# Attention with a gated feed-forward block on one core: 32-column tiles for values and row sums, batch 0 masked by TensorE, loads and output matmuls moved

## The chip, the cores and the metric

The kernel runs on one core of a Trainium2 chip. The metric is the device time of one execution in microseconds (us). The traces were taken by the hardware profiler; PE is TensorE's matmuls, PEld its weight loads, DVE VectorE, ACT ScalarE, POOL GpSimd, SP SyncE. The granted clock (PEclk in the views) is the share of TensorE's full clock that the profiler records as let through. PSUM is the memory in which the matmuls leave their results, in banks.

## The reference

```python
def _attn_ref(q, k, v, beacon_k, beacon_v):          # B, H, S, Nb, D = 8, 8, 576, 16, 64
    k_all = np.concatenate([beacon_k, k], axis=2)
    v_all = np.concatenate([beacon_v, v], axis=2)
    scores = scale * np.matmul(q, k_all.transpose(0, 1, 3, 2))
    causal[:, Nb:] = np.triu(np.ones((S, S), dtype=bool), k=1)
    scores = np.where(causal, -1e9, scores)
    a = softmax(scores)                              # written out in the original
    return np.matmul(a, v_all)

def _moe_ref(x, w_gate, w_val, w_out):               # x: 4608 x 512, d_ff = 1536
    return (gelu(x @ w_gate) * (x @ w_val)) @ w_out
```

The output of attention, 8 heads of 64 side by side, is `x`. Inputs and output are float32 in memory; the matmuls are in bf16.

## The kernel before

A batch has four pairs of heads. For each pair, the scores are made in four chunks (0 to 3) in a ring of two PSUM buffers; ScalarE takes the exponential of each; GpSimd masks the diagonal. Then TensorE multiplies with the values and, with a tile of ones, makes row sums. After attention, 12 gate/value tiles of 8 matmuls follow. The 48 output matmuls of a batch are those of the chunk of tokens before it, and they are strewn in bursts `o(n)` over attention, to keep TensorE busy while ScalarE works.

```python
    psum_s: bufs=2, two banks each    # scores, gate/value
    psum_x: bufs=1, three banks       # values and row sums; also output tile 0 of a batch
    psum_o: bufs=1, one bank          # output tiles 1, 2 and 3 of a batch
# ... (cut; a summary of the pools, not the code's own lines)

    def out_mms(ci, u0, u1, wide=lambda ti: False):
        for u in range(u0, u1):
            ti, fi = divmod(u, F_TILES)              # F_TILES = 12: an output tile is 12 matmuls
            # ... (cut)
            if fi == 0:
                if wide(ti):
                    o_of[ci][1] = psum_x.tile([P, 1536], FP32, name="o_ps", tag="x")[:, 0:D_MODEL]
                else:
                    o_of[ci][1] = psum_o.tile([P, D_MODEL], FP32, name="o_ps", tag="o")
            # ... (cut: the matmul)
            if fi == F_TILES - 1:
                keep(nc.vector.tensor_copy(o_sb[:, ti, :], o_ps))
                # ... (cut: the store)

    # batches 1 to 7; ab(m): score chunks 0 and 1 of pair m, cd(m): chunks 2 and 3,
    # av(m): values, row sums and normalization
            o(6)
            ab(0)
            o(10)
            cd(0)
            o(8)
            for m in range(1, NPAIR):
                ab(m)
                av(m - 1)
                cd(m)
                o(6 if m < NPAIR - 1 else 5)
            av(3, direct=True)
            o(7)
        # ... (cut)
        for fi in range(F_TILES):
            gate_val(b, fi, kk_late=fi == 0)
```

`keep` holds each engine's instructions to the order written.

The softmax here doesn't subtract the row's maximum and nothing guards it: scores larger than these inputs give would overflow.

## Time and profile before

| | before |
|---|---|
| time, median | 398.4 us (398.1 to 399.1) |
| TensorE busy | 97% of the span |
| one batch (first gate matmul to the next batch's) | 42.2 us |
| gate/value matmuls in it | 20.8 us |
| values and row sums of one pair | 1.56 us |

The first fence is from the page of the kernel before: the span, the busy time of the engines with their share of the span, and the granted TensorE clock in tenths over 40 slices.

```profile
span 396.2 us, 7413 instructions
PE 382.3 (97%) x3046; PEld 185.9 (47%) x3046; DVE 190.5 (48%) x304; ACT 202.2 (51%) x280; POOL 156.3 (39%) x277
...
PEclk9999999999999999999999999999999999999999
...
PE 79%; DMA 8%; POOL 3%; DVE 3%; ACT 3%; issue 2%; SPq 2%; POOLq 0%; ACTq 0%
```

The last line is the chain of waits: four fifths of it is TensorE itself. A window over one batch of the same kernel shows that TensorE does not rest there at all: 42.20 us busy in 42.20 us.

```profile
core 0: us, PE busy (x) PEld busy (x) DVE busy (x) ACT busy (x) POOL busy (x), PEclk, DMA share, GB/s
76.44:118.64 42.20, 42.20 (x338) 20.37 (x337) 21.17 (x33) 23.99 (x33) 21.02 (x38) 1.00 0.99 97
```

### The profile page before, as it was taken

How to read it: one execution, taken by the hardware profiler on the slowest of the kernel's cores; microseconds unless marked ns; L12 is line 12 of the kernel's file. 1: busy time of each engine (PE TensorE's matmuls, PEld its weight loads, DVE VectorE, ACT ScalarE, POOL GpSimd, SP SyncE). 2: the span in 40 equal slices, each digit the busy share in tenths (PEclk: the TensorE clock that was granted, in tenths of full speed). 3: DMA queues.
4: the chain of work that ended last, by engine and by line, in shares of the span. 5: the costliest groups of instructions: out<-in, count | busy, mean ns of one | idle time of the engine just before them, and what ended most of it. 6: DMA issues, size and time to landing. Idle time of an engine off the chain costs nothing.

```text
span 396.2 us, 7413 instructions
## 1 busy us (share of the span) xinstructions
PE 382.3 (97%) x3046; PEld 185.9 (47%) x3046; DVE 190.5 (48%) x304; ACT 202.2 (51%) x280; POOL 156.3 (39%) x277
## 2 busy tenths in 40 slices
PE   3889999999999999999999999999999999999996
PEld 2464545544454445444544455444544455444442
DVE  1393654844375327642673338433754266332332
ACT  2775258634873379336843586347823793332210
POOL 8722395780369124931486047803400240000000
PEclk9999999999999999999999999999999999999999
DMA  7999998699129930996099915991032010000012
GB/s 91 180 206 204 175 132 97 68 169 121 55 36 156 141 79 30 120 156 84 29 107 162 89 55 57 163 137 58 28 89 59 34 45 32 0 0 29 28 53 106
DMA packets 139154, 36.24 MB, mean 91 GB/s; under 512 B 126832, under 2 KB 134512, under 8 KB 139120
## 3 DMA queue, kind: packets, MB, share of 16 engines
q0 software_dynamic: 103984, 19.14, 64.4%
q1 hardware_dynamic: 35136, 16.62, 19.3%
q8 instruction: 24, 0.39, 0.4%
q14 instruction: 10, 0.08, 0.1%
HBM read 38.27 MB, written 9.44 MB: 120 GB/s over the span
## 4 chain that ended last, share of the span: by engine, by line
PE 79%; DMA 8%; POOL 3%; DVE 3%; ACT 3%; issue 2%; SPq 2%; POOLq 0%; ACTq 0%
PE gv_ps L155 36%; PE o_ps L155 23%; PE x_ps L155 11%; PE s_ps L155 8%; DMA qkT<-k_sb_94 3%; DMA v_sb_98<-in_beacon_v_dram 2%; SPq L196 2%; ACT expT L158 2%; DMA k_sb_97<-in_k_dram 2%; POOL k_sb_97 L109 1%; PE t_ps L167 1%; DVE qkT L178 1%; POOL q_sb_96 L109 1%; PE w_ps L155 1%; DMA kb<-in_beacon_k_dram 1%
## 5 line engine op out<-in xcount | busy, mean ns | idle before, releaser
L158 ACT ACTIVATE ge_sb<-gv_ps 128x512 bf16<-128x512 f32 x108 | 64.5, 597 | 150.7 <-PE gv_ps L155 150.7
L340 DVE TENSOR_TENSOR hT_sb<-gv_ps,ge_sb 128x512 bf16<-128x512 f32 x108 | 74.7, 692 | 116.0 <-ACT ge_sb L158 116.0
L158 ACT ACTIVATE expT<-s_ps 128x1024 bf16<-128x1024 f32 (+3 forms) x128 | 103.9, 870 | 25.8 <-PE s_ps L155 25.7
L155 PE MATMUL gv_ps<-xT_sb,wg_sb 128*128 128x512 bf16 x432 | 112.2, 379 | 0.8 <-DVE xT_sb L312 0.8
L155 PE MATMUL gv_ps<-xT_sb,wv_sb 128*128 128x512 bf16 x432 | 112.2, 379 | 0.0
L238 POOL TENSOR_SCALAR_AFFINE_SELECT expT<-expT 128x256 bf16<-128x256 bf16 (+2 forms) x140 | 52.4, 388 | 142.2 <-ACT expT L158 142.1
L155 PE MATMUL o_ps<-wo_sb,hT_sb 128*128 128x512 bf16 x432 | 103.6, 380 | 0.0
L155 PEld LDWEIGHTS <-wv_sb 128*128 128x128 bf16 x432 | 42.3, 98 | 52.7 <-issue 2.7
L155 PEld LDWEIGHTS <-wg_sb 128*128 128x128 bf16 x432 | 41.9, 98 | 49.9
L155 PEld LDWEIGHTS <-hT_sb 128*128 128x128 bf16 x432 | 38.8, 98 | 46.6 <-issue 2.8
L364 DVE COPY o_sb<-o_ps 128x512 f32<-128x512 f32 x36 | 24.7, 687 | 37.9 <-PE o_ps L155 37.9
L155 PE MATMUL s_ps<-qkT 64*128 64x80 bf16 (+5 forms) x384 | 39.1, 294 | 2.7 <-DVE qkT L183 1.5
L155 PE MATMUL x_ps<-expT,ones 128*64 128x432 bf16 (+1 forms) x558 | 41.2, 243 | 0.0
L304 DVE STREAM_TRANSPOSE zT_sb<-x_ps 128x576 f32<-128x576 f32 x29 | 22.7, 781 | 29.9 <-ACT x_sb L158 29.9
L155 PEld LDWEIGHTS <-qkT 64*128 64x128 bf16 x384 | 14.8, 96 | 30.4 <-issue 21.8
L155 PEld LDWEIGHTS <-ones 128*64 128x64 bf16 (+1 forms) x578 | 23.2, 110 | 4.6
L307 DVE STREAM_TRANSPOSE rec_sb<-r_sb 128x576 f32<-128x576 f32 x29 | 22.6, 778 | 1.0
L155 PE MATMUL x_ps<-expT,v_sb_95 128*64 128x80 bf16 (+5 forms) x270 | 21.5, 245 | 1.5 <-DVE zT_sb L304 1.1
L155 PE MATMUL x_ps<-expT,v_sb_98 128*64 128x80 bf16 (+5 forms) x288 | 22.8, 246 | 0.0
L109 POOL DMA_DIRECT2D v_sb_98<-in_v_dram x20 | 17.0, 868 | 11.9 <-DMA wv_sb<-in_moe_w_val_dram 3.7
L109 POOL DMA_DIRECT2D v_sb_95<-in_v_dram x20 | 17.0, 889 | 2.5 <-DMA k_sb_94<-in_k_dram 2.3
L312 DVE TENSOR_TENSOR xT_sb<-x_sb,rec_sb 128x576 bf16<-128x576 f32 x23 | 17.4, 758 | 0.9
(51 smaller groups left out, 190.9 us busy)
## 6 DMA issues: line engine op xcount, KB each, us to landing
out_dram<-o_sb SPq DMA_DIRECT2D x36, 256.0 KB, 2.0
v_sb_95<-in_v_dram POOLq DMA_DIRECT2D x12, 128.0 KB, 7.9
wg_sb<-in_moe_w_gate_dram POOLq DMA_DIRECT2D x3, 512.0 KB, 11.6
wv_sb<-in_moe_w_val_dram POOLq DMA_DIRECT2D x3, 512.0 KB, 13.3
wo_sb<-in_moe_w_out_dram POOLq DMA_DIRECT2D x1, 1536.0 KB, 23.5
v_sb_98<-in_v_dram POOLq DMA_DIRECT2D x12, 128.0 KB, 10.6
q_sb_93<-in_q_dram POOLq DMA_DIRECT2D x12, 128.0 KB, 4.2
q_sb_96<-in_q_dram POOLq DMA_DIRECT2D x12, 128.0 KB, 4.2
```

What stands on the lines that cost most here:

```text
L109: keep(nc.gpsimd.dma_start(out=out_ap, in_=in_ap))
L155: keep(nc.tensor.matmul(out_ap, lhsT, rhs, start=start, stop=stop, **kw))
L158: keep(nc.scalar.activation(out_ap, in_ap, func, **kw))
L167: keep(nc.tensor.transpose(out_ap, in_ap, ident[0:n, 0:n]))
L178: nc.vector.tensor_copy(qkT[:, m, :, NB:SK].rearrange("p w (t r) -> p w t r", r=6), t_ps[:, 0:2, 0:S].rearrange("p w (r t) -> p w t r", r=6),)
L196: nc.sync.dma_start_transpose(out=qkT[:, :, w, c + j * P : c + j * P + n], in_=src[0:n, j, :, :].rearrange("p h d -> p (h d)"),)
L238: nc.gpsimd.affine_select(out=d, in_=d, pattern=[[0, 2], [1, n]], compare_op=ALU.is_ge, fill=0.0, base=NB if t == 0 else 0, channel_multip ...
L304: keep(nc.vector.transpose(zT_sb, z_ps))
L307: nc.vector.transpose(rec_sb.rearrange("p (c o) -> p c o", o=32), r_sb.to_broadcast([P, S // 32, 32]))
L312: nc.vector.tensor_tensor(out=xT_sb[:, m, b * S : (b + 1) * S], in0=x_sb, in1=rec_sb, op=ALU.mult)
L340: nc.vector.tensor_tensor(out=h_of[ci][:, fi, :], in0=gv_ps[:, 1, :], in1=ge_sb, op=ALU.mult)
L364: keep(nc.vector.tensor_copy(o_sb[:, ti, :], o_ps))
```

## The change

Its intent, as the code shows it:

- Row sums need only 32 columns of ones, so four 32-column tiles are meant to work at once on two heads and two ranges of queries. Values use four 32-column tiles too. Row sums get a bank of their own (`psum_z`), and the division reads values from PSUM, without ScalarE's copy.
- The rows of `x` are then in another order, so the gate and value weights are loaded in quarters, 24 loads in place of 6, and the third pair of weights comes after batch 1's queries and keys.
- Batch 0: TensorE adds a large negative number above the diagonal; VectorE's masks and ten warming matmuls go.
- The last two gate/value tiles of a batch do both gates first, so that the GELUs end sooner.
- The output matmuls are shared out anew: 14, not 24, before the second pair.

```diff
+ZS = 352
+Z_ORDER = [(0, 0), (0, 1), (1, 1), (1, 0), (2, 1), (2, 0), (3, 1), (4, 1)]
...                                                  (row sums, batches 1 to 7)
+            for t, u in Z_ORDER:
+                lo, end = (ZS, S) if u else (0, ZS)
+                for hi in range(2):
+                    p0 = 64 * u + 32 * hi
+                    mm(z_ps[p0 : p0 + 32, q0 - lo : end - lo], ones[0 : KROWS[t], 0:32], ...)
...                                                  (values: r = 0 to 3, 32 columns each)
+                for r in range(4):
+                    mm(x_ps[32 * r : 32 * r + 32, X0 + q0 : X0 + q1], v_sb[..., 32 * (r // 2) : 32 * (r // 2) + 32], ...)
...                                                  (loads)
-    for i in range(3):
-        load_gate_val(i)
+    load_gate_val(0)
+    load_gate_val(1)
     load_qk6(1, 0, H)
     load_kb(1)
+    load_gate_val(2)
     load_out_w()
...                                                  (batches 1 to 7)
+            o(4)
+            ab(0)
             o(6)
-            ab(0)
-            o(10)
             cd(0)
-            o(8)
+            o(4)
             for m in range(1, NPAIR):
                 ab(m)
                 av(m - 1)
                 cd(m)
-                o(6 if m < NPAIR - 1 else 5)
-            av(3, direct=True)
-            o(7)
+                o(8)
+            av(3)
+            o(10)
...                                                  (gate/value)
-            gate_val(b, fi, kk_late=fi == 0)
+            if fi < F_TILES - 2:
+                gate_val(b, fi, kk_late=fi == 0)
+            elif fi == F_TILES - 2:
+                gate_val_pair(b, fi)
```

(Cut: the masks of batch 0, the order of its pairs, and the normalization's four small reciprocals.)

More of the change, by code (lines that the diff above doesn't have):

```diff
@@ L38 @@
 AV_ORDER = [0, 2, 4, 1, 3]
-X0 = 16
-Z0 = X0 + S
+X0 = 512 - S_LO[4]
+ZS = 352
+Z_ORDER = [(0, 0), (0, 1), (1, 1), (1, 0), (2, 1), (2, 0), (3, 1), (4, 1)]
 QK_SCALE = 0.125
@@ L77 @@
     psum_x = ctx.enter_context(tc.tile_pool(name="psum_x", bufs=1, space=bass.MemoryType.PSUM))
+    psum_z = ctx.enter_context(tc.tile_pool(name="psum_z", bufs=1, space=bass.MemoryType.PSUM))
     psum_o = ctx.enter_context(tc.tile_pool(name="psum_o", bufs=1, space=bass.MemoryType.PSUM))
@@ L100 @@
     nc.vector.memset(qkT[:, :, 1, SK:640], 0.0)
-    tri = const.tile([P, P], BF16, name="tri", tag="tri")
-    nc.vector.memset(tri, 3e38)
+    behind = const.tile([P, P], BF16, name="behind", tag="behind")
+    nc.vector.memset(behind, -3e38)
     def dma(out_ap, in_ap):
@@ L148, in load_gate_val @@
         for w, dst in ((moe_w_gate, wg_sb), (moe_w_val, wv_sb)):
-            keep(nc.gpsimd.dma_start(out=dst[:, :, fs], in_=w[:, fs].rearrange("(kk p) f -> p kk f", p=P)))
+            for g in range(4):
+                a, c = g % 2, g // 2
+                dma(
+                    dst[32 * g : 32 * g + 32, :, fs],
+                    w[:, fs].rearrange("(kk q p) f -> q p kk f", q=4, p=32)[2 * a + c],
+                )
     def load_out_w():
@@ L161, in transpose_pe @@
     def transpose_pe(b, m, pool, tag):
-        t_ps = pool.tile([P, 3 if tag == "x" else 2, 1024], BF16, name="t_ps", tag=tag)
+        t_ps = pool.tile([P, 2, 1024], BF16, name="t_ps", tag=tag)
         qk, kb = qk6[b]
@@ L183, in transpose_pe @@
         keep(nc.vector.tensor_copy(qkT[:, m, 1, 0:NB], t_ps[:, 1, S:SK]))
-    def warm(b, m, n):
-        w_ps = psum_o.tile([P, D_MODEL], FP32, name="w_ps", tag="o")
-        for _ in range(n):
-            mm(w_ps, ident, qkT[:, m, 1, 0:512], True, True)
     def transpose_dma(b):
@@ L209, in scores @@
         s_ps = psum_s.tile([P, 2, 512], FP32, name="s_ps", tag="s")
-        for t, s_lo, w, col in CHUNKS[c]:
+        for j, (t, s_lo, w, col) in enumerate(CHUNKS[c]):
             for hi in range(2):
@@ L216, in scores @@
                     qkT[r, m, 0, NB + s_lo : NB + s_lo + w],
+                    j == 0,
                     True,
-                    True,
+                    skip_group_check=True,
                 )
+        if b == 0:
+            for t, s_lo, w, col in CHUNKS[c]:
+                if s_lo == S_LO[t]:
+                    n, q0 = DIAG[t], NB if t == 0 else 0
+                    for hi in range(2):
+                        mm(
+                            s_ps[:, hi, col : col + n],
+                            behind,
+                            ident[:, q0 : q0 + n],
+                            False,
+                            True,
+                            skip_group_check=True,
+                        )
         o, w = CHUNK_OFF[c], CHUNK_W[c]
@@ L231, in masks @@
             d = expT[0 : KROWS[t], :, EXP_OFF[t] : EXP_OFF[t] + n]
-            if b == 0:
-                w = tri[0 : KROWS[t], NB : NB + n] if t == 0 else tri[0 : KROWS[t], 0:n]
-                w = w.rearrange("p (o n) -> p o n", o=1).to_broadcast([KROWS[t], 2, n])
-                keep(nc.vector.tensor_tensor(out=d, in0=d, in1=w, op=ALU.min))
-            else:
-                keep(
-                    nc.gpsimd.affine_select(
-                        out=d,
-                        in_=d,
-                        pattern=[[0, 2], [1, n]],
-                        compare_op=ALU.is_ge,
-                        fill=0.0,
-                        base=NB if t == 0 else 0,
-                        channel_multiplier=-1,
-                    )
-                )
@@ L251 @@
-    x_of = {}
-    def attend(b, m, t, wide=False):
-        i = b * NPAIR + m
-        if t == AV_ORDER[0]:
-            if wide:
-                x_of[i] = tuple(
-                    (psum_s.tile([P, 1024], FP32, name=name, tag="s"), 0, 512) for name in ("xs_ps", "zs_ps")
-                )
-            else:
-                x_ps = psum_x.tile([P, 1536], FP32, name="x_ps", tag="x")
-                x_of[i] = ((x_ps, X0, 512 - X0), (x_ps, Z0, 1024 - Z0))
-        expT, v_sb = exp_of[i], v_ring[b % NRING]
-        kr, first, last = KROWS[t], t == AV_ORDER[0], t == AV_ORDER[-1]
-        for w, (ps, base, split) in enumerate(x_of[i]):
-            for q0, q1 in ((S_LO[t], split), (max(split, S_LO[t]), S)):
+            keep(
+                nc.gpsimd.affine_select(
+                    out=d,
+                    in_=d,
+                    pattern=[[0, 2], [1, n]],
+                    compare_op=ALU.is_ge,
+                    fill=0.0,
+                    base=NB if t == 0 else 0,
+                    channel_multiplier=-1,
+                )
+            )
@@ new lines, with attend @@
+    x_of = {}
+    def attend(b, m, x_in, by_act):
+        i = b * NPAIR + m
+        expT, v_sb = exp_of[i], v_ring[b % NRING]
+        if by_act:
+            z_ps = psum_s.tile([P, 1024], FP32, name="z_ps", tag="s")
+            for t in AV_ORDER:
+                for q0, q1 in ((S_LO[t], 512), (max(512, S_LO[t]), S)):
+                    e0 = EXP_OFF[t] + q0 - S_LO[t]
+                    for r in range(4):
+                        mm(
+                            z_ps[32 * r : 32 * r + 32, q0:q1],
+                            ones[0 : KROWS[t], 0:32],
+                            expT[0 : KROWS[t], r % 2, e0 : e0 + q1 - q0],
+                            t == AV_ORDER[0],
+                            t == AV_ORDER[-1],
+                            skip_group_check=True,
+                        )
+        else:
+            z_ps = psum_z.tile([P, 512], FP32, name="z_ps", tag="z")
+            for t, u in Z_ORDER:
+                lo, end = (ZS, S) if u else (0, ZS)
+                q0 = max(lo, S_LO[t])
+                e0 = EXP_OFF[t] + q0 - S_LO[t]
+                for hi in range(2):
+                    p0 = 64 * u + 32 * hi
+                    mm(
+                        z_ps[p0 : p0 + 32, q0 - lo : end - lo],
+                        ones[0 : KROWS[t], 0:32],
+                        expT[0 : KROWS[t], hi, e0 : e0 + end - q0],
+                        t == 0,
+                        t == (4 if u else 2),
+                        skip_group_check=True,
+                    )
+        pool, tag = x_in
+        x_ps = pool.tile([P, 1024], FP32, name="x_ps", tag=tag)
+        for t in AV_ORDER:
+            for q0, q1 in ((S_LO[t], S_LO[4]), (max(S_LO[4], S_LO[t]), S)):
@@ L269, in attend @@
                 e0 = EXP_OFF[t] + q0 - S_LO[t]
-                for hi in range(2):
+                for r in range(4):
                     mm(
-                        ps[64 * hi : 64 * hi + 64, base + q0 : base + q1],
-                        ones[0:kr, :] if w else v_sb[0:kr, t, 2 * m + hi, :],
-                        expT[0:kr, hi, e0 : e0 + q1 - q0],
-                        first and (wide or not (w == 1 and q0 == 0)),
-                        last,
+                        x_ps[32 * r : 32 * r + 32, X0 + q0 : X0 + q1],
+                        v_sb[0 : KROWS[t], t, 2 * m + r % 2, 32 * (r // 2) : 32 * (r // 2) + 32],
+                        expT[0 : KROWS[t], r % 2, e0 : e0 + q1 - q0],
+                        t == AV_ORDER[0],
+                        t == AV_ORDER[-1],
@@ L277, in attend, with normalize @@
                         skip_group_check=True,
                     )
-    def normalize(b, m, by_act=False, direct=False):
+        x_of[i] = x_ps[:, X0 : X0 + S], z_ps
+    def normalize(b, m, by_act):
         i = b * NPAIR + m
-        (x_ps, xc, _), (z_ps, zc, _) = x_of.pop(i)
-        x_ps, z_ps = x_ps[:, xc : xc + S], z_ps[:, zc : zc + S]
+        x_ps, z_ps = x_of.pop(i)
         del exp_of[i]
         rec_sb = npool.tile([P, S], FP32, name="rec_sb", tag="rec_sb")
-        x_sb = x_ps
-        if not direct:
-            x_sb = npool.tile([P, S], FP32, name="x_sb", tag="x_sb")
@@ L293, in normalize @@
         if by_act:
-            ln_sb = npool.tile([P, S], FP32, name="ln_sb", tag="zT_sb")
-            act(ln_sb, z_ps, ACT.Ln)
-            if not direct:
-                keep(nc.vector.tensor_copy(x_sb, x_ps))
+            ln_sb = npool.tile([P, S], FP32, name="ln_sb", tag="ln_sb")
+            act(ln_sb, z_ps[:, 0:S], ACT.Ln)
             act(rec_sb, ln_sb, ACT.Exp, scale=-1.0)
         else:
-            zT_sb = npool.tile([P, S], FP32, name="zT_sb", tag="zT_sb")
+            zT_sb = npool.tile([P, ZS], FP32, name="zT_sb", tag="zT_sb")
@@ L301, in normalize @@
             r_sb = npool.tile([P, S // 32, 1], FP32, name="r_sb", tag="r_sb")
-            if not direct:
-                act(x_sb, x_ps, ACT.Copy)
-            keep(nc.vector.transpose(zT_sb, z_ps))
-            keep(nc.vector.reciprocal(r_sb, zT_sb.rearrange("p (c o) -> p c o", o=32)[:, :, 0:1]))
+            n, w = ZS // 32, S - ZS
+            keep(nc.vector.transpose(zT_sb[:, 0:w], z_ps[:, 0:w]))
+            keep(nc.vector.transpose(zT_sb[0:64, w:ZS], z_ps[0:64, w:ZS]))
+            z = zT_sb.rearrange("p (c o) -> p c o", o=32)[:, :, 0:1]
@@ L306, in normalize @@
+            for p in (64, 0):
+                keep(nc.vector.reciprocal(r_sb[p : p + 64, n:, :], z[64:P, 0 : w // 32, :]))
+            for p in (0, 64):
+                keep(nc.vector.reciprocal(r_sb[p : p + 64, 0:n, :], z[0:64, :, :]))
             keep(
@@ L312, in normalize @@
             nc.vector.tensor_tensor(
-                out=xT_sb[:, m, b * S : (b + 1) * S], in0=x_sb, in1=rec_sb, op=ALU.mult
+                out=xT_sb[:, m, b * S : (b + 1) * S], in0=x_ps, in1=rec_sb, op=ALU.mult
             )
@@ L318, with feed_tile, gv_mm, gelu @@
     h_of, o_of = {}, {}
-    def gate_val(ci, fi, kk_late=False):
+    def feed_tile(ci, fi):
         if fi == 0:
             h_of[ci] = hpool.tile([P, F_TILES, CH], BF16, name="hT_sb", tag="hT_sb")
-        n0 = ci * CH
-        gv_ps = psum_s.tile([P, 2, CH], FP32, name="gv_ps", tag="s")
-        order = [(w, kk) for w in range(2) for kk in range(K_CHUNKS)]
-        if kk_late:
-            order.sort(key=lambda t: t[1] == K_CHUNKS - 1)
-        for w, kk in order:
-            mm(
-                gv_ps[:, w, :],
-                (wg_sb, wv_sb)[w][:, kk, fi * P : (fi + 1) * P],
-                xT_sb[:, kk, n0 : n0 + CH],
-                kk == 0,
-                kk == K_CHUNKS - 1,
-                skip_group_check=True,
-            )
+        return psum_s.tile([P, 2, CH], FP32, name="gv_ps", tag="s")
+    def gv_mm(gv_ps, ci, fi, w, kk):
+        mm(
+            gv_ps[:, w, :],
+            (wg_sb, wv_sb)[w][:, kk, fi * P : (fi + 1) * P],
+            xT_sb[:, kk, ci * CH : (ci + 1) * CH],
+            kk == 0,
+            kk == K_CHUNKS - 1,
+            skip_group_check=True,
+        )
+    def gelu(gv_ps):
         ge_sb = fpool.tile([P, CH], BF16, name="ge_sb", tag="ge_sb")
         act(ge_sb, gv_ps[:, 0, :], ACT.Gelu)
+        return ge_sb
+    def product(ci, fi, gv_ps, ge_sb):
         keep(
@@ L343, in gate_val, with gate_val_pair @@
         )
+    def gate_val(ci, fi, kk_late=False):
+        gv_ps = feed_tile(ci, fi)
+        order = [(w, kk) for w in range(2) for kk in range(K_CHUNKS)]
+        if kk_late:
+            order.sort(key=lambda t: t[1] == K_CHUNKS - 1)
+        for w, kk in order:
+            gv_mm(gv_ps, ci, fi, w, kk)
+        product(ci, fi, gv_ps, gelu(gv_ps))
+    def gate_val_pair(ci, f0):
+        tiles = [feed_tile(ci, f0), feed_tile(ci, f0 + 1)]
+        ge = []
+        for i, gv_ps in enumerate(tiles):
+            for kk in range(K_CHUNKS):
+                gv_mm(gv_ps, ci, f0 + i, 0, kk)
+            ge.append(gelu(gv_ps))
+        for i, gv_ps in enumerate(tiles):
+            for kk in range(K_CHUNKS):
+                gv_mm(gv_ps, ci, f0 + i, 1, kk)
+            product(ci, f0 + i, gv_ps, ge[i])
     def out_mms(ci, u0, u1, wide=lambda ti: False):
@@ L351, in out_mms @@
                 if wide(ti):
-                    o_of[ci][1] = psum_x.tile([P, 1536], FP32, name="o_ps", tag="x")[:, 0:D_MODEL]
+                    o_of[ci][1] = psum_z.tile([P, D_MODEL], FP32, name="o_ps", tag="z")
                 else:
@@ L378 @@
     load_kb(0)
+    by_diagonal(behind, ALU.is_gt, 0.0)
     load_qk6(0, 2, 4)
     load_qk6(0, 4, H)
-    by_diagonal(tri, ALU.is_ge, 0.0)
     load_v(0)
-    for i in range(3):
-        load_gate_val(i)
+    load_gate_val(0)
+    load_gate_val(1)
     load_qk6(1, 0, H)
     load_kb(1)
+    load_gate_val(2)
     load_out_w()
@@ L404, in cd, with av @@
             scores(b, m, 3)
-        def av(m, wide=False, **kw):
-            for t in AV_ORDER:
-                attend(b, m, t, wide)
-            normalize(b, m, **kw)
+        def av(m, by_act=False, x_in=(psum_x, "x")):
+            attend(b, m, x_in, by_act)
+            normalize(b, m, by_act)
         keep(nc.scalar.preload_act_table_set(SET_EXP))
         if b == 0:
-            for m in range(NPAIR):
-                ab(m)
-                if m == NPAIR - 1:
-                    for mm_ in (0, 1, 2):
-                        for c in range(4):
-                            if (mm_, c) > (1, 1):
-                                masks(0, mm_, c)
-                    av(0)
-                    for c in (0, 1):
-                        masks(0, m, c)
-                else:
-                    transpose_pe(0, m + 1, psum_x, "x")
-                    if m == 2:
-                        for mm_, c in ((0, 0), (0, 1), (0, 2), (0, 3), (1, 0), (1, 1)):
-                            masks(0, mm_, c)
-                cd(m)
-                if 1 <= m < NPAIR - 1:
-                    warm(b, m, 5)
-            for c in (2, 3):
-                masks(0, NPAIR - 1, c)
-            av(1, by_act=True)
-            av(2, wide=True, by_act=True, direct=True)
-            av(3, by_act=True, direct=True)
-        else:
-            o(6)
-            ab(0)
-            o(10)
+            ab(0)
+            transpose_pe(0, 1, psum_x, "x")
+            cd(0)
+            ab(1)
+            transpose_pe(0, 2, psum_x, "x")
+            cd(1)
+            transpose_pe(0, 3, psum_x, "x")
+            ab(2)
+            cd(2)
+            av(0)
+            ab(3)
+            cd(3)
+            av(1)
+            av(2, by_act=True, x_in=(psum_s, "s"))
+            av(3, by_act=True)
+        else:
+            o(4)
+            ab(0)
+            o(6)
             cd(0)
-            o(8)
+            o(4)
             for m in range(1, NPAIR):
```

## The prediction

> **What bounds it.** The page shows TensorE busy 97% of 396.2 us at clock 1.0; the chain of waits puts 79% on it. Read from the timeline, one batch takes 42.18 us: 20.83 gate/value matmuls, 10.35 output matmuls (48 x 0.2157), about 6.2 values and row sums (4 pairs x 1.56), 3.7 scores, the rest gaps of about 0.1 us where the tiling mode changes ([...]last output matmul's slot ends 98.57, scores start 98.67).
>
> **What changes on TensorE.** Row sums now stream about 960 columns in four 32-column groups instead of 1664 in two. Estimate from the measured 1.56 us for 3328 columns: 1.3 us per pair if four groups overlap. That is 0.25 us x 30 pairs = 7.5 us of TensorE work removed.
>
> **Why little of it reaches the span.** A second loop runs through ScalarE. The two score buffers make the fourth score chunk wait for the second exponential: from the start of a pair's scores, 0.49 to the first exponential, two exponentials 1.89, 0.05 back = 2.43 us. In between TensorE has only scores 0.53, values 1.56 and third chunk 0.2; it already waits about 0.12 us there. With 1.3 us it waits about 0.36. So three of four pairs gain nothing; only the last does. Removing ScalarE's copy (0.66) does not help: it comes after the second exponential. I estimate attention at 21.4 us per batch, as before (21.36).
>
> **What is added.** The paired last two gate/value tiles take both score buffers at once. The last tile's gate needs the buffer of tile 9, whose product ends 1.52 us after tile 9's matmuls (timeline), but only 0.86 us of gate matmuls stand between: a new wait of about 0.7 us per batch, 7 counted batches: +5 us. The earlier GELU merely lets ten output matmuls move later, conserving work.
>
> **Batch 0.** Masks leave VectorE, the ten warming matmuls go, loads of the exponential loop tighten: gate/value of batch 0 should start 3 to 4 us earlier (29.6 before for the first). But batch 1's masks on GpSimd follow its DMA issues in order; those waited until 47.0 us for the output weights to land, and its first mask came at 59.95, just in time. DMA was busy throughout, bytes are equal, and 24 small weight loads replace 6 (each issue 0.5 us or more). So the first mask cannot come before about 60 to 62; TensorE stalls 3 to 4 us before batch 1's first values, with 10 fewer output matmuls done. Net +0.5 to +3 us. DMA transposes, which cost about 1 us of waits in later batches, start about 1 us earlier: -1.
>
> **Sum.** 398.4 + 5 + 1.5 - 1, and perhaps -1 for the last pairs: about 403 us; range 395.5 to 409. Chances: faster by over 2% 0.07, within 2% 0.73, slower 0.20.
>
> **What will show it.** Values plus row sums per pair: near 1.3 us. Fourth score chunk: wait on ScalarE about 0.35 us in three pairs of a batch. Gate matmuls: wait on VectorE's product, 7 or 8 times, about 0.7 us each. Gate/value of batch 0 starts at about 28 us; batch 1's first values wait for GpSimd's mask until past 61. Batch period about 42.7.
>
> **What would make it wrong.** If four column groups do not overlap[...], values exceed 1.6 us and every pair pays: slower. If weights land sooner in small pieces, GpSimd is free earlier and the 3 to 4 us of the opening stay gained. If the paired tiles' wait is hidden, the result is about 398. A longer VectorE chain (four reciprocals, division straight from PSUM) could hold the single value buffer and stall the next pair.

## More of the kernel before

The next fence is from the timeline of the kernel before, in the first part of a batch: start, length, engine, line, operation, tiles, count, and in brackets the idle time before it with what ended it.

```profile
101.86 1.90 PE L155 MATMUL o_ps<-wo_sb,hT_sb 128*128 128x512 bf16 x8
103.69 0.60 PE L155 MATMUL s_ps<-qkT 64*128 64x512 bf16 x8
103.80 0.69 DVE L364 COPY o_sb<-o_ps 128x512 f32<-128x512 f32 x1 [2.40 <-PE o_ps L155]
...
106.32 0.61 PE L155 MATMUL o_ps<-wo_sb,hT_sb 128*128 128x512 bf16 x2
```

The burst of 8 ends with the 24th output matmul of the batch. VectorE copies the finished tile out while TensorE makes scores and values, and the next burst comes 2.6 us after the last one ended.

## The result, and the profile after

The changed kernel takes 434.9 us (median of 4 runs, 432.6 to 437.0) against 398.3 us: slower, with a ratio of 1.092 (95% interval 1.085 to 1.099). The ratio is the mean time of one kernel's fast runs over that of the other's fast runs in the same rounds, so it is not quite the ratio of the medians. I had said 403, with a range that ended at 409.

The page of the changed kernel, the same lines:

```profile
span 434.3 us, 8696 instructions
PE 385.0 (89%) x3583; PEld 188.7 (43%) x3632; DVE 199.3 (46%) x406; ACT 189.4 (44%) x256; POOL 164.9 (38%) x295
...
PEclk9999998999989998999999999999899989999999
...
PE 71%; DVE 15%; ACT 7%; issue 3%; POOL 2%; DMA 1%; DVEq 0%; ACTq 0%; POOLq 0%
```

TensorE is busy for as long as before (385 against 382 us) in a span 38 us longer; VectorE is now 15% of the chain, and five slices are below the full clock. Two batches in windows:

```profile
85.00:132.07 47.07, 42.15 (x395) 20.28 (x399) 22.54 (x49) 22.34 (x30) 20.83 (x38) 0.96 0.94 87
132.07:179.43 47.36, 42.44 (x395) 20.47 (x400) 22.68 (x49) 22.44 (x30) 21.23 (x38) 0.96 0.92 86
```

A batch has grown by 5 us, with a granted clock of 0.96 and TensorE idle for nearly 5 us, 4.1 us of it in waits (the rest is in part matmuls whose records are missing). The waits of the whole changed kernel, longest in total first (who waited for whom, us, times, longest), show what is new:

```profile
PE o_ps L167 <- DVE o_sb L424: 19.9, 14, 1.8
...
PE s_ps L167 <- ACT expT L170: 5.8, 20, 0.5
...
PE gv_ps L167 <- DVE hT_sb L378: 4.2, 8, 0.6
...
PE z_ps L167 <- POOL expT L253: 2.1, 2, 1.5
```

In the kernel before, the first of these has no line at all. The timeline of the changed kernel shows one of the 14 waits:

```profile
118.02 0.78 DVE L343 STREAM_TRANSPOSE rec_sb<-r_sb 128x576 f32<-128x576 f32 x1
118.16 0.38 PE L167 MATMUL o_ps<-wo_sb,hT_sb 128*128 128x512 bf16 x1 [0.16 <-issue]
...
118.91 0.76 DVE L348 TENSOR_TENSOR xT_sb<-x_ps,rec_sb 128x576 bf16<-128x576 f32 x1
119.58 0.68 DVE L424 COPY o_sb<-o_ps 128x512 f32<-128x512 f32 x1
120.31 2.72 PE L167 MATMUL o_ps<-wo_sb,hT_sb 128*128 128x512 bf16 x6 [1.77 <-DVE o_sb L424]
```

Two of a burst of 8 output matmuls, the 23rd and 24th, are done by 118.5 (the record of the 23rd is missing). The 25th starts the next output tile, which has the same single bank, so it must wait until VectorE has copied the tile out. In VectorE's order the normalization of the pair stands before the copy. And the six matmuls after the wait take 2.72 us; six take 1.46 us at full clock (bursts of six elsewhere in both traces).

The reason is in the count. Output tiles end at matmuls 12, 24, 36 and 48. The bursts of the kernel before end at 6, 16, **24**, 30, **36**, 41, 48: the ends of tiles 1 and 2 coincide with ends of bursts, and other work follows. Those of the changed kernel end at 4, 10, 14, 22, 30, 38, 48: 24 and 36 lie inside bursts of 8. (The end at 12 lies inside a burst in both, but the first tile of a batch has another bank.)

### The profile page after: what moved, and what is told of

Read it like the earlier page. It is cut to its first block, busy times and chain, and to the rows that moved or that the text cites. A ratio compares the mean times of both kernels' runs of the same rounds, so it can differ in the third digit from the quotient of the medians.

```text
span 434.3 us, 8696 instructions
## 1 busy us (share of the span) xinstructions
PE 385.0 (89%) x3583; PEld 188.7 (43%) x3632; DVE 199.3 (46%) x406; ACT 189.4 (44%) x256; POOL 164.9 (38%) x295
## 4 chain that ended last, share of the span: by engine, by line
PE 71%; DVE 15%; ACT 7%; issue 3%; POOL 2%; DMA 1%; DVEq 0%; ACTq 0%; POOLq 0%
PE gv_ps L167 41%; PE o_ps L167 18%; ACT expT L170 6%; PE s_ps L167 6%; PE z_ps L167 3%; DVE rec_sb L343 3%; DVE xT_sb L348 3%; DVE o_sb L424 2%; PE x_ps L167 2%; DVE hT_sb L378 2%; DVE r_sb L341 2%; DVE zT_sb L335 1%; DVE r_sb L339 1%; PE t_ps L179 1%; ACT ge_sb L170 1%
## 5 line engine op out<-in xcount | busy, mean ns | idle before, releaser
L170 ACT ACTIVATE expT<-s_ps 128x1024 bf16<-128x1024 f32 (+3 forms) x128 | 101.7, 865 | 66.1 <-PE s_ps L167 65.8
L167 PE MATMUL s_ps<-qkT 64*128 64x80 bf16 (+5 forms) x384 | 43.8, 307 | 8.3 <-ACT expT L170 5.8
L335 DVE STREAM_TRANSPOSE zT_sb<-z_ps 128x224 f32<-128x224 f32 x30 | 12.5, 417 | 57.2 <-PE z_ps L167 57.2
L115 POOL DMA_DIRECT2D v_sb<-in_v_dram x40 | 33.9, 881 | 6.2 <-DMA k_sb<-in_k_dram 5.6
L167 PE MATMUL x_ps<-expT,v_sb 128*32 128x80 bf16 (+5 forms) x1152 | 33.3, 248 | 0.1
L167 PEld LDWEIGHTS <-v_sb 128*32 128x32 bf16 (+1 forms) x1152 | 29.5, 99 | 0.7 <-issue 0.3
L115 POOL DMA_DIRECT2D q_sb<-in_q_dram x30 | 25.3, 860 | 7.4 <-DMA wo_sb<-in_moe_w_out_dram 7.1
L115 POOL DMA_DIRECT2D k_sb<-in_k_dram x30 | 25.4, 891 | 2.1 <-DMA q_sb<-in_q_dram 2.1
L348 DVE TENSOR_TENSOR xT_sb<-x_ps,rec_sb 128x576 bf16<-128x576 f32 x32 | 24.1, 757 | 3.8 <-ACT rec_sb L170 0.7
L167 PE MATMUL z_ps<-expT,ones 128*32 128x224 bf16 (+11 forms) x560 | 21.3, 261 | 2.1 <-POOL expT L253 2.1
```

Of the source, the lines that this page charges most:

```text
L115: keep(nc.gpsimd.dma_start(out=out_ap, in_=in_ap))
L167: keep(nc.tensor.matmul(out_ap, lhsT, rhs, start=start, stop=stop, **kw))
L170: keep(nc.scalar.activation(out_ap, in_ap, func, **kw))
L335: keep(nc.vector.transpose(zT_sb[:, 0:w], z_ps[:, 0:w]))
L348: nc.vector.tensor_tensor(out=xT_sb[:, m, b * S : (b + 1) * S], in0=x_ps, in1=rec_sb, op=ALU.mult)
```

## The experiments

Times are medians; "before" in each group is the same kernel before, 397.7 to 398.2 us in these rounds. All kernels gave correct results.

### after_old_split: the changed kernel with the old bursts

```diff
-            o(4)
+            o(6)
             ab(0)
-            o(6)
+            o(10)
             cd(0)
-            o(4)
+            o(8)
 ...
-                o(8)
+                o((0, 6, 6, 5)[m])
             av(3)
-            o(10)
+            o(7)
```

> The changed kernel with the kernel before's split of the output matmuls (6, 10, 8, then 6, 6, 5, then 7), nothing else. Theory BOUNDARY: in the changed split the 24th and 36th output matmul, where an output tile ends, fall in the middle of a burst of 8, and the next tile has the same single PSUM buffer, so TensorE waits for VectorE's copy (1.8 and 0.9 us per batch) and then runs some matmuls at half clock. With the old split the boundaries fall at the ends of bursts: 434.9 falls by 25 to 28 us, to 405 to 411, and the waits for o_sb (19.9 us) go to under 1 us. Rival ATTENTION: the 32-column tiles and the longer VectorE chain are what is slow; then it stays over 425.

Measured: 403.7 us (403.0 to 404.7), ratio 1.015 (1.013 to 1.018). The waits for `o_sb` are gone from the list and the mean granted clock is 1.00. The sharing out of output matmuls is therefore worth 31 us of the 36.6 us, somewhat more than the 25 to 28 that I expected. Two batches in windows, with the columns as above:

```profile
78.30:120.96 42.66, 40.75 (x396) 19.81 (x401) 22.74 (x48) 22.36 (x30) 20.93 (x37) 1.00 1.09 96
120.96:163.65 42.69, 40.78 (x395) 19.78 (x400) 22.73 (x49) 22.36 (x30) 21.17 (x39) 1.00 1.05 96
```

TensorE is busy for 1.4 us less per batch than before (40.75 against 42.20), but in part because six records of matmuls are missing here; in after_three_undone, where none of these is, it is 41.12 us, so 32-column tiles save about 1.1 us. Yet a batch is not shorter: 1.3 us of waits came with it, for exponentials (0.8) and for a gate/value product (0.5). That is the rest of the prediction, and it is taken up below.

### before_new_split: the kernel before with the new bursts

```diff
-            o(6)
+            o(4)
             ab(0)
-            o(10)
+            o(6)
             cd(0)
-            o(8)
+            o(4)
 ...
-                o(6 if m < NPAIR - 1 else 5)
+                o(8)
             av(3, direct=True)
-            o(7)
+            o(10)
```

> The kernel before with the changed kernel's split of the output matmuls (4, 6, 4, then 8, 8, 8, then 10), nothing else. BOUNDARY: slower by 12 to 25 us (two waits a batch of 0.7 to 1.6 us, with half-clock matmuls after), waits of TensorE for o_sb appear, 10 us or more in all. ATTENTION: within 3 us of the kernel before.

Measured: 460.6 us (459.6 to 461.8), ratio 1.159 (1.155 to 1.162). The direction was right and the size far over what I expected. From the waits and two windows of this run:

```profile
PE o_ps L155 <- DVE o_sb L364: 37.6, 14, 3.1
```

```profile
core 0: us, PE busy (x), PEclk, DMA share, GB/s
324.80:328.00 3.20, 0.15 (x1) 0.81 0.00 0
328.00:330.60 2.60, 2.58 (x6) 0.50 0.27 101
330.60:333.60 3.00, 3.00 (x33) 0.50 0.00 0
```

The same bursts cost the kernel before 63 us and the changed one 31 us. In the kernel before the copy stands behind a normalization that itself waits longer: first for ScalarE's copy of the values, then come a transpose of 0.78 us and three more instructions:

```profile
324.68 0.78 DVE L304 STREAM_TRANSPOSE zT_sb<-x_ps 128x576 f32<-128x576 f32 x1 [1.77 <-ACT x_sb L158]
...
327.28 0.68 DVE L364 COPY o_sb<-o_ps 128x512 f32<-128x512 f32 x1
```

Its longest wait is 3.1 us, against 1.8 us, and the clock then reads half for 5.6 us (328.0 to 333.6). So the rest of the change is not what made the bursts costly; it softens them.

### after_block_split: light front, but whole tiles

```diff
             o(4)
             ab(0)
             o(6)
             cd(0)
-            o(4)
+            o(2)
 ...
-                o(8)
+                o((0, 12, 12, 6)[m])
             av(3)
-            o(10)
+            o(6)
```

> The changed kernel with another split of the output matmuls: 4, 6, 2, then 12, 12, 6, then 6. The front of a batch stays as light as in the change (12 instead of 14, against 24 in the kernel before), but every output tile ends at the end of a burst. BOUNDARY: waits for o_sb vanish (under 1 us in all) and the time is 403 to 412. Rival FRONT: what hurt was taking ten output matmuls away from the front of a batch; then it stays over 425, and if both, between.

Measured: 410.5 us (409.7 to 410.7), ratio 1.031. No wait for `o_sb` is listed. This tells the two readings of the split apart: with only 12 output matmuls in front, even fewer than in the change, the large loss is gone as soon as tiles end with bursts. What remains, 7 us over after_old_split, is the most that FRONT can account for; its batches are 42.97 us against 42.66, and its opening is 4 us longer, with 2.7 us of waits for batch 1's masks (0.6 us in after_old_split).

### after_dummies: the same waits with TensorE kept busy

```diff
+            if fi == 0 and ti >= 2 and not wide(2):
+                d_ps = psum_z.tile([P, D_MODEL], FP32, name="d_ps", tag="z")
+                for _ in range(7 if ti == 2 else 3):
+                    mm(d_ps, ident, wo_sb[:, 0, :], True, True)
```

> The changed kernel with useless matmuls (7 and 3 of 512 columns, into the idle row-sum bank) just before the output tiles that start inside a burst, so that TensorE is busy while it waits for VectorE's copy. They shorten no wait; they only keep TensorE active. Theory CLOCK: part of the 31 us is that TensorE's clock is halved after the idle stretch (granted 0.50 in the six matmuls after it); then the granted clock goes back to about 1.0 and the time falls by 6 to 10 us, to 425 to 429, with the rest of the loss still there. Rival: the waits alone are the loss; then the same within 1 us, or slower.

Measured: 429.6 us (426.1 to 431.6), ratio 1.079 (1.074 to 1.085), 5 us less than the changed kernel, just short of what I expected. The windows of the changed kernel around the wait, and those of this one:

```profile
113.30:116.70 3.40, 3.24 (x55) 1.00 0.00 0
116.70:120.10 3.40, 1.41 (x31) 0.97 0.00 0
120.10:123.50 3.40, 3.19 (x12) 0.52 0.20 77
```

```profile
118.00:121.20 3.20, 2.56 (x18) 1.00 0.00 0
121.20:122.70 1.50, 1.45 (x8) 1.00 0.43 160
```

The six matmuls after the wait, from this run's timeline:

```profile
121.25 1.46 PE L167 MATMUL o_ps<-wo_sb,hT_sb 128*128 128x512 bf16 x6 [0.27 <-DVE o_sb L428]
```

Useless matmuls, which shorten no wait, keep the clock full here: 1.46 us, where the changed kernel took 2.72. By the traces, every batch of after_dummies takes 45.78 us, and the batches of the changed kernel take 47.2 to 47.4 us, but for one of 45.78. So in a batch the waits cost 3.1 us (45.78 less the 42.66 of after_old_split) and the half clock 1.5 us where it comes. That it comes in some batches and not in others goes with the spread of 1%: the changed kernel's two runs at a mean clock of 0.976 took 436.4 and 437.0 us, the two at 0.982 and 0.984 took 432.6 and 433.3. The waits are two thirds of the loss; the clock is the rest. The run gave a little of its gain back, since its opening had a longer wait for masks (3.6 us in all).

What halves the clock is shown only in part. The six matmuls after the wait took 2.72 us, against 1.46, at a granted clock of 0.50 (120.30 to 122.90 us). The longest gap before them was 1.77 us, and TensorE was busy for 1.41 us between 116.70 and 120.10. The longest gap alone does not decide: in batch 1 of the changed kernel a wait of 1.83 us, up to 74.54 us, was followed by six matmuls in 1.46 us. And some batches escape: one in six in the changed kernel, three in six in after_no_pair and in after_gates_first. What does decide is not shown.

### after_no_pair: the last two gate/value tiles one after the other

```diff
-            if fi < F_TILES - 2:
-                gate_val(b, fi, kk_late=fi == 0)
-            elif fi == F_TILES - 2:
-                gate_val_pair(b, fi)
+            gate_val(b, fi, kk_late=fi == 0)
```

> The changed kernel with the last two gate/value tiles done one after the other, as before. If the pair's wait for tile 9's product (0.55 us, 8 times, measured) is a plain loss: faster by about 4 us and no wait of gate matmuls for hT_sb. If the earlier GELU and table load pay for it: same or slower, because the first exponential of a batch then starts about 0.7 us later relative to the end of the gate/value matmuls.

Measured: 433.8 us (433.0 to 435.8), no clear difference from 434.9. The gate matmuls' wait for `hT_sb` is gone from the list, yet batches without a clock dip take 45.74 us against 45.78. So with the new bursts the pair's wait (0.55 us) is real and is paid back: without the pair, TensorE waits at the front of a batch, 0.23 us for the last product and 0.38 us for an exponential (near 201 to 204 us), and with it not. With the old bursts it is not paid back: batches fall from 42.66 us in after_old_split to 41.95 in after_three_undone (below), which has no pair. There, 6 and 10 output matmuls (1.46 and 2.33 us in the kernel before) already cover the GELU (0.60 us) and ScalarE's table load (1.28 us).

### after_gates_first: the third weight load back in front

```diff
     load_gate_val(1)
+    load_gate_val(2)
     load_qk6(1, 0, H)
     load_kb(1)
-    load_gate_val(2)
```

> The changed kernel with the third gate/value weight load back before batch 1's queries and keys. Theory WINDOW: at most eight loads are outstanding, each issue waits for the eighth before it, and the two large loads in the middle of the small ones let DMA run dry (69 to 112 GB/s around 36 to 42 us); with the small ones together wo_sb lands 1.5 to 3 us earlier than 50.1, the first GpSimd mask comes at 60 to 61.5 instead of 63.0, and the time falls by 1 to 3 us. Rival: the 24 small loads themselves are slow; then wo_sb still lands at about 50 and nothing changes.

Measured: 431.4 us (429.9 to 433.1), 3.5 us less than the changed kernel; since clock dips vary, the events are the better measure. From the timelines of GpSimd, the changed kernel first and then this one:

```profile
50.14 3.32 POOL L115 DMA_DIRECT2D q_sb<-in_q_dram  x4 [7.12 <-DMA wo_sb<-in_moe_w_out_dram]
...
62.96 2.72 POOL L253 TENSOR_SCALAR_AFFINE_SELECT expT<-expT 128x224 bf16<-128x224 bf16 x8
```

```profile
47.97 3.31 POOL L115 DMA_DIRECT2D q_sb<-in_q_dram  x4 [6.73 <-DMA wo_sb<-in_moe_w_out_dram]
...
60.60 1.83 POOL L253 TENSOR_SCALAR_AFFINE_SELECT expT<-expT 128x224 bf16<-128x224 bf16 x5
```

The output weights land 2.2 us earlier and the first mask of batch 1 comes 2.4 us earlier. (Before: 47.3 and 59.95.) TensorE's wait for masks in batch 1, 2.1 us, is no longer listed. The order was the fault, not the 24 loads as such, whose issues took 0.54 to 0.57 us each. In the traces of the opening, issues that wait are released, by the names there, by the landing of the load eight places before: all 11 in the kernel before, after waits of 0.7 to 6.2 us. In the changed kernel two of the last small loads waited 3.6 and 2.8 us in this way for batch 1's queries and keys, and the output weights behind them were issued at 36.39 us, against 31.58 here. DMA moved 69 to 177 GB/s between 36 and 42 us, and 176 on average from 24 to 50 us, against 188 here. That DMA ran dry is not shown: in that stretch its engines were busy for 0.8 or more of the time, but for one slice of 0.65 us.

### after_three_undone: old bursts, no pair, old order of loads

The edits of after_old_split, after_no_pair and after_gates_first together; 32-column tiles, the normalization and batch 0 stay changed.

> The changed kernel with the old split, the last two gate/value tiles one after the other, and the third weight load first: what is left of the change is the 32-column tiles, the normalization and batch 0. If the costs add: 403.7 less 3 to 4 (pair) less 2 to 3 (loads) = 396 to 399. If 32-column tiles shortened the chain by the 0.3 us per pair that they save on TensorE, 30 pairs, it would be about 390. I expect 397, because the fourth score chunk's wait on ScalarE takes it back in three pairs of four: waits of scores for expT 6 us or more.

Measured: 398.0 us (397.7 to 398.2), ratio 1.000 (0.998 to 1.001). The costs add: the three undone parts are the whole loss, and what remains is neutral. By the trace, a batch takes 41.95 us (before: 42.2 to 42.5), but the opening ends 1.4 us later than before. TensorE's waits of scores for ScalarE are 6.8 us:

```profile
PE s_ps L167 <- ACT expT L170: 6.8, 24, 0.5
```

### tiles_filled: two output matmuls before the third score chunk

The diffs from here to tiles_fill_between are against after_three_undone; that of tiles_filled_early is against tiles_filled.

```diff
                 ab(m)
                 av(m - 1)
+                o(2)
                 cd(m)
-                o((0, 6, 6, 5)[m])
+                o((0, 4, 4, 3)[m])
```

> after_three_undone with two of each pair's output matmuls moved between the values and the third score chunk (2 then 4, 4, 3). Theory LOOP: the time from a pair's first scores to its fourth chunk is fixed by two exponentials, 2.4 us, and the saved 0.3 us becomes time only if TensorE has other work in there; then each of three pairs falls from 4.02 to about 3.7 us, 5 to 7 us in all: about 391, and the waits of scores for expT in the pairs vanish. Rival: the switch between tiling modes added per pair, or the DMA transposes, which were just in time, take it back: 396 or more.

Measured: 398.8 us (398.6 to 399.1). No gain; this expectation failed. The first filled pair did fall to 3.7 us (105.11 to 108.84 in the trace of the next run, which has the same bursts), but the later ones took 3.9. With the third chunk pushed back, ScalarE had nothing to do for 0.55 us, and then its four exponentials in a row (3.37 us) held the next pair's scores. I had moved a wait from TensorE to ScalarE. What a switch between tiling modes adds was not measured apart; the prediction read a gap of 0.10 us at one.

### tiles_filled_early: the same, with transposes earlier and one load later

```diff
+            if NPERM <= b + 1 < B:
+                transpose_dma(b + 1)
             av(3)
             o(7)
 ...                                   (cut: the old call of transpose_dma goes, load_v(2) moves from batch 0 to batch 1)
```

> tiles_filled with the DMA transposes of the next batch issued before the last values of a batch instead of after its first gate tile, and batch 2's values loaded a batch later, so that GpSimd is free for batch 1's masks about 5 us earlier. If DMA transposes or the GpSimd queue hold tiles_filled, it is 2 to 4 us faster than that; if not, the same within 1 us.

Measured: 398.5 us (398.3 to 398.9), the same as without: neither the DMA transposes nor GpSimd's queue held it.

### tiles_fill_between: two output matmuls between the third and the fourth chunk

```diff
                 av(m - 1)
-                cd(m)
-                o((0, 6, 6, 5)[m])
+                scores(b, m, 2)
+                o(2)
+                scores(b, m, 3)
+                o((0, 4, 4, 3)[m])
```

> after_three_undone with two output matmuls between a pair's third and fourth score chunk, not ahead of the third. In tiles_filled the third chunk came too late for ScalarE, which then idled 0.55 us a pair. Here the third exponential can follow the second at once: pairs of 3.8 us against 4.02, 4 to 5 us in all: 393 to 395. Rival: ScalarE's four exponentials (3.27 us) plus TensorE's mode switches set about 3.95 a pair whatever the order: 397 to 399.

Measured: 394.8 us (394.4 to 395.1), ratio 0.993 (0.992 to 0.994), and 3.2 us less than after_three_undone (2.6 by the two ratios to the kernel before, since they ran in different rounds). It is faster than both kernels, if only by 0.7%. The timeline shows a pair of 3.79 us, from 109.05 to 112.84, without a wait at the fourth chunk (the record of the second of the two output matmuls is missing):

```profile
109.05 0.60 PE L167 MATMUL s_ps<-qkT 64*128 64x512 bf16 x8
109.54 3.13 ACT L170 ACTIVATE expT<-s_ps 128x1024 bf16<-128x1024 f32 x4 [0.66 <-PE s_ps L167]
...
110.83 0.37 PE L167 MATMUL s_ps<-qkT 64*128 64x464 bf16 x2
111.36 0.38 PE L167 MATMUL o_ps<-wo_sb,hT_sb 128*128 128x512 bf16 x1 [0.16 <-issue]
...
111.67 0.26 PE L167 MATMUL s_ps<-qkT 64*128 64x208 bf16 x2
111.87 1.04 PE L167 MATMUL o_ps<-wo_sb,hT_sb 128*128 128x512 bf16 x4
112.84 0.60 PE L167 MATMUL s_ps<-qkT 64*128 64x512 bf16 x8
```

So the loop through ScalarE is what kept the work saved by 32-column tiles from becoming time, and work in the right place of it lets part of the saving through.

### tiles_fill_warm and tiles_fill_rewarm: the opening

Both add to tiles_fill_between the earlier transposes and the later load. The first also has nine matmuls of zeros before the first data; the second has eight full-array matmuls after batch 0's second pair instead.

```diff
+    # ... (cut in both: the tiles w_ps and wz)
+    for _ in range(9):                              # tiles_fill_warm, before the first transposes
+        mm(w_ps, wz[:, 0:P], wz, True, True)
 ...
+            for _ in range(8):                      # tiles_fill_rewarm, after batch 0's second pair
+                mm(w_ps, ident, qkT[:, 1, 1, 0:512], True, True)
```

> tiles_fill_between with batch 2's values loaded a batch later, the DMA transposes issued earlier, and nine matmuls of zeros before the first data arrive, so that batch 0 does not run at half clock. If the half clock of the first 24 us and GpSimd's first mask hold the opening: gate/value matmuls of batch 1 start 1.5 to 3 us earlier than in tiles_fill_between and the time falls by as much. If the idle gaps of batch 0 bring the half clock back: no gain.

> tiles_fill_warm without the nine matmuls at the start; instead eight full-array matmuls of 512 columns after batch 0's second pair, as the kernel before had five there. Theory: those removed matmuls were what brought the clock to full rate in batch 0 (the kernel before ran at full rate from about 17 us, the changed one at half rate until 24 us although TensorE was busy 97% from 15 to 24 us with small and transposing matmuls). Then the matmuls after them run at full rate, and gate/value matmuls of batch 0 start 0.5 to 2 us earlier than 32.3. Rival: batch 0 is bound by its chain through ScalarE and VectorE; then the start stays at 32 or later, since the eight take 2 to 3.4 us themselves.

Measured: 394.4 us (394.0 to 394.6) and 395.0 us (394.7 to 396.2): no gain worth telling from 394.8. The zeros brought the clock up for the first 24 transposes only (0.70 us at 5.26 us); within batch 0, whose longest gap was 1.52 us, it fell back (1.17 us for the next 24, from 9.37 us). (By its matmuls' durations the kernel before reached full rate at 18 to 19 us, not at 17.) The eight matmuls did bring it up for good (the transposes after them take 0.70 us for 24, against 1.17), but the first gate matmul came at 32.88 us, not earlier than the 32.78 of tiles_fill_between.

```profile
17.28 2.99 PE L167 MATMUL w_ps<-qkT,ident 128*128 128x512 bf16 x8
20.20 0.70 PE L179 MATMUL t_ps<-ident,qk 96*64 96x96 bf16 x24
```

This does not show that half clock is harmless. The eight put the transposes after them off by 2.5 us (20.20 against 17.68 in tiles_fill_between), and all but 0.1 us of that was made up by the first gate matmul: the full clock gave back about what raising it cost. Nor can a few tenths be read here: with the same batch 0, the first gate matmul came at 31.9 to 32.8 us in the changed kernel and four runs made from it. How much of the opening is half clock, what else holds it, and how its 1.4 us could be had back, stay open.

Busy time alone did not raise the clock in the opening: in the changed kernel TensorE was busy for 8.77 of the 9 us from 15 to 24 us, with transposes, score matmuls of 64 rows and small masking matmuls, and still ran at half rate (1.17 us for 24 transposes). In that stretch the profile records a granted clock of 1.00, so in the opening I go by the matmuls' durations. In tiles_fill_warm, where the clock had risen and fallen before, the record of 15 to 25 us reads 0.50.

## Why the prediction was right or wrong

**Wrong: one step, and it was the large one.** The step reads: "The earlier GELU merely lets ten output matmuls move later, conserving work." It took output matmuls for filling that can be poured anywhere. They come in tiles of 12 that share one bank, and where a tile ends inside a burst, TensorE waits for VectorE. Put back alone, the bursts give 31 us of the 36.6; put alone into the kernel before, they cost it 63 us. The step missed the wait (about 3.1 us per batch) and, after it, the half clock (about 1.5 us in most batches). The prediction's list of what could make it wrong named a longer VectorE chain and a single buffer, but of the values; the bank that mattered was the one of the output tiles. Not tried were a second bank for the output tiles, and the copy placed before the normalization in VectorE's order; what either would give is not known.

**Right, tiles.** Values and row sums take 1.25 us per pair in the changed kernel (111.38 to 112.63; 52 matmuls, each with its own weight load, against 1.56 us for 36 in two column tiles), where I said 1.3. By estimate about 3.4 tiles worked at once: the 52 matmuls stream 9984 columns in 1.25 us, and one output matmul takes 0.216 us for 512. TensorE's work fell by about 1.1 us per batch, where four pairs of 0.25 make 1.0.

**Right, why it does not reach the span.** The fourth chunk waits 0.28 us where I said 0.36. With the three other parts undone the change is neutral, and filling the loop at the right place gave about 3 us.

**Right in the wait, half right in its price: the pair.** I said 0.7 us per batch; 0.55 us was measured, 8 times. With the new bursts it costs nothing net; with the old ones a batch is 0.71 us longer. That the old-bursts kernel lands at 403.7, next to the predicted 403, is because the terms of the sum, the output matmuls apart, were about right in size. For the opening that was luck: its +1.5 was to come from an early start and then a stall of 3 to 4 us for masks; in after_old_split it came to 1.9 us, from a late start with a stall of 0.6.

**Wrong, batch 0's start.** I said 3 to 4 us earlier than 29.6; it came at 32.3. Without the warming matmuls TensorE stayed at half clock until 24 us (24 transposes took 1.17 us, against 0.70 after the eight matmuls of tiles_fill_rewarm), and the estimate had no term for that. How much of the miss it explains is not known, since the matmuls that restored the clock cost about as much as it gave back. It mattered little, as I had expected GpSimd's masks in batch 1 to be the later limit.

**Nearly right, GpSimd's first mask.** I said 60 to 62; it came at 62.96, and 2.4 us of that are the order of the loads. TensorE waited 2.1 us for masks, where I said 3 to 4. I had allowed for the number of loads, not for their order.

## What to carry to other kernels

When work is moved to fill gaps, look at where its accumulation buffers turn over: with a single PSUM bank, as here, every end of a tile needs a stretch of other work behind it that is longer than the copy and all that stands before the copy in its engine's queue. Here the copy took 0.68 us; without such a stretch the waits were 1.8 us at most with a normalization of eight VectorE instructions ahead, and up to 3.1 us where that chain waited for ScalarE first. A list of waits with no entry for some buffer may mean that a careful order hides the wait, so count what holds it before changing the order. And in this kernel, work saved on the busiest engine did not become time by itself inside a loop that another engine closes (398.0 us in after_three_undone, 394.8 in tiles_fill_between). In such a loop, find the place where the saved time appears as a wait, and move other work exactly there.
